# One change in four places of a spectral-gating kernel: warm-up matmuls, late tables, filter gathers and the last product

## The chip, the cores and the metric

The kernel runs on one core of a Trainium2 chip. The metric is device microseconds of one execution. Every timed execution comes with the span of the core and the mean clock that TensorE was granted (1.0 is full speed), and one execution of each kernel is kept as a full trace. Executions of a kernel can fall in a slower state; all named here are of the fast state unless the text says otherwise, and a single execution has no state of its own.

One thing has to be said at the start, because the whole reading hangs on it: after the first measurement, the five batches of experiments fell on five different chips (numbered 4, 15, 7, 12 and 1), and the kernel before is about 10 us slower on some of them than on others. The number of the first chip was not recorded. Each chip was met in one batch only, so the chip can't be told from the hour; "a chip with late marks", below, is short for both. Ratios are therefore always taken against the kernel before **on the same chip in the same rounds**.

## The reference

```python
def reference(A_x, A_w_r, A_w_i, ..., B_w_gate, B_w_up, B_w_down):   # cut
    x  = A_x                                  # [1, 2048, 640]
    xn = layernorm(x)
    X  = rfft2(xn) * (w_r + 1j * w_i)         # filter of 2048 x 321
    s  = irfft2(X)
    g  = silu((gelu(xn @ w_gate) * (xn @ w_up)) @ w_down)   # 640 -> 1536 -> 640
    return x + s * g
```

The two branches share TensorE. The feed-forward branch gives it most of its work. The spectral branch is a chain of small products with copies and multiplications between them; after its first stage it writes its data to DRAM and reads it back in another order (the *regroup*, four loads of 0.66 MB), and it multiplies by filter rows that are fetched in eight groups, G = 0 to 7.

## The kernel before

All instructions are first put in a plan (`add` with an engine, a cost, an order and what it must follow); a list scheduler then fixes the order on each engine, so a change in one place can move instructions elsewhere. The parts that the change touches:

```python
def keep_warm(e):                        # 12 dummy matmuls on constants
    place(heat, (2, 512))
    for k in range(12):
        nc.tensor.matmul(heat.tile[:, k % 2, :], lhsT=idle.tile[:, 0:P], rhs=idle.tile, ...)
...
def gather(G):                           # filter rows of group G, four gathers on GpSimd
    def go(e):
        sw.tile = WF[G % 3]              # three buffers: groups 0, 1, 2 need not wait
        for pm in range(2):              # row k, and its mirror row (2048 - k) % 2048
            for ri, wsrc in enumerate((A_w_r, A_w_i)):
                nc.gpsimd.indirect_dma_start(out=sw.tile[:, pm, ri, 0:L], in_=wsrc,
                    in_offset=bass.IndirectOffsetOnAxis(ap=LANE[:, 2 * G + pm:...], axis=0))
    W_in[G] = add(go, "POOL", ..., after=[stored[7]] + ([W_in[G - 1]] if G else []), new=[sw])
...
for k in ("ti", "i1", "im", "it"):       # late tables: SyncE, directly behind the regroup
    load_tab(k, (0, 1, seq[0]), after=[B_in["go"]])
...
# last product: two column pieces, 384 and 256 wide; per piece tanh on ScalarE, then
# (product * y), (tanh + 1) * that, + x  on VectorE, and a store
for lo, hi, tag in ((0, 384, "pg"), (384, 640, "pu")) if last else ...:
```

Of the kernel before, what the change touches and what calls it, by code (L numbers as in the profile page):

```python
# [11 lines left out]
FP32 = mybir.dt.float32  # L12
# [121 lines left out]
class Plan:  # L134
# [6 lines left out]
    def __init__(self, bufs, free):  # L141
        self.bufs, self.free = bufs, dict(free)
        self.tasks, self.slots = [], {t: [] for t in bufs}
        self.wire = 2200.0
# [84 lines left out]
def kernel(  # L229
# [33 lines left out]
    warm = consts.tile([P, 1], FP32)  # L263
    STAT = consts.tile([P, NSLAB, 12], FP32)
# [57 lines left out]
    def load_tab(k, rank=None, after=()):  # L322
        seq[0] += 1
        tab_in[k] = dma(flat(tiles[k]), tabs[k], rank or (0, -4, seq[0]), int(np.prod(tiles[k].shape)) * 2, after=after)
# [18 lines left out]
    nc.scalar.dma_start(out=X[:, 1, :], in_=xv[:, 1, :])  # L343
    nc.scalar.activation(out=warm, in_=warm, func=ACT.Gelu_apprx_tanh)
# [8 lines left out]
    def keep_warm(e):  # L353
        place(heat, (2, 512))
        for k in range(12):
            nc.tensor.matmul(heat.tile[:, k % 2, :], lhsT=idle.tile[:, 0:P], rhs=idle.tile, start=True, stop=True, skip_group_check=True)
    t = add(blank, "DVE", (330, 400), (0, -9), new=[idle])
    add(keep_warm, "PE", (12 * 430, 12 * 430), (0, -9), after=[t], new=[heat], use=[idle])
# [3 lines left out]
    load_tab("id")  # L362
    load_x(3, 4)
# [19 lines left out]
    def stats(n1, engs):  # L383
        x = X[:, n1, :]
        mean, var, rstd = MVA[:, n1, 0:1], MVA[:, n1, 1:2], RSTD[:, n1, :]
        costs = {"DVE": (1000, 1200), "ACT": (1900, 2050)}
        junk = Slot("th")

        def first(e):
            if e == "DVE":  # L390
                for g in range(2):
                    nc.vector.bn_stats(out=STAT[:, n1, 6 * g:6 * g + 6], in_=x[:, 320 * g:320 * g + 320])  # L392
                nc.vector.bn_aggr(out=MVA[:, n1, :], in_=STAT[:, n1, :].rearrange("p (g s) -> p g s", g=2))
                nc.vector.tensor_scalar_add(out=var, in0=var, scalar1=1e-5)  # L394
                return
            j = place(junk, (D,))
            nc.scalar.activation(out=j, in_=x, func=ACT.Copy, scale=-1.0 / D, accum_out=NM[:, n1, :])
            nc.scalar.activation(out=j, in_=x, func=ACT.Square, scale=1.0, bias=NM[:, n1, :], accum_out=var)

        eng = engs[0]  # L400
        t = add(first, eng, costs[eng], (2, n1), after=[x_in[n1]] + ([aps[3]] if n1 > 3 else []), new=[junk] if eng == "ACT" else [], use=[sX])
# [8 lines left out]
    def apply(n1, root, new):  # L410
# [8 lines left out]
        return add(go, "DVE", (360, 510), (1, n1, 0), hold=350 if n1 < 4 else 0, after=[root], new=[sxn] if new else [], use=[sX] if new else [sX, sxn])  # L419
# [109 lines left out]
    def gather(G):  # L529
        sw = Slot("W")  # L530

        def go(e):
            sw.tile = WF[G % 3]
            for pm in range(2):
# [4 lines left out]
        W_in[G] = add(go, "POOL", (4200, 4200), (3, G), after=[stored[7]] + ([W_in[G - 1]] if G else []), new=[sw],  # L539
# [6 lines left out]
    for k in ("ti", "i1", "im", "it"):  # L546
        load_tab(k, (0, 1, seq[0]), after=[B_in["go"]])
# [4 lines left out]
    def spectral(G):  # L552
# [34 lines left out]
        z_done = add(cp, either(1024), None, (1, 101 + 10 * G), after=[a], use=[pz, sZ])  # L587
        sE, es, firsts = Slot("ma"), [], []
# [170 lines left out]
    def gate_up(grp, t):  # L759
# [28 lines left out]
        a = add(act, "ACT", c_act(512), (0, step[0]), after=[last[id(Wg)]], new=[ge], use=[pg])  # L788
# [10 lines left out]
    def down(n1):  # L799
# [7 lines left out]
        for lo, hi, tag in ((0, 384, "pg"), (384, 640, "pu")) if last else ((0, 320, "pg"), (320, 640, "pu")):  # L807
# [13 lines left out]
            def tanh(e, lo=lo, hi=hi, ps=ps, th=th):  # L821
                place(th, (320 if not last else 384,), FP32)
                nc.scalar.activation(out=th.tile[:, 0:hi - lo], in_=ps.tile[:, 0:hi - lo], func=ACT.Tanh, scale=0.5)  # L823
# [83 lines left out]
```

## Time and profile before

| | kernel before |
|---|---|
| time, three runs before the change | 218.37 to 219.92 us, median 219.0 |
| span of the profiled run | 216.9 us |
| TensorE busy | 202.5 us, 93% of the span |
| VectorE busy | 164.0 us, 76% |
| ScalarE busy | 104.2 us, 48% |
| mean granted clock | 0.975 |

The busy shares alone say "TensorE"; they do not say where its 14 idle microseconds and its time at half clock lie. The prediction below goes through the slices, the stretches and the chain to find them. In the views PE is TensorE, PEld its weight loads, DVE VectorE, ACT ScalarE, POOL GpSimd and SP SyncE. One view that the prediction tells but does not show is GpSimd's timeline. Its columns are start, duration, engine, line, operation, output and input, and in brackets the idle time ahead of it with its cause:

```profile
43.57 1.09 POOL L536 DMA_INDIRECT WF<-in_A_w_r_dram,LANE  x1 [0.18 <-issue]
...
57.49 0.95 POOL L536 DMA_INDIRECT WF<-in_A_w_i_dram,LANE  x1 [0.30 <-issue]
```

These are the first and the last of twelve gathers that stand in a row, one every 1.25 us, from 43.6 to 58.4 us.

### The profile page before, as it was taken

To read this page: it belongs to the slowest core of one execution; us is meant where nothing else is said; L and a number is where in the kernel's file an instruction comes from. 1 tells how busy PE (TensorE), PEld (TensorE's weight loads), DVE (VectorE), ACT (ScalarE), POOL (GpSimd) and SP (SyncE) were. 2 spreads that over 40 slices of the span, in tenths; PEclk is the share of its full clock that TensorE was granted. 3 is DMA by queue.
4 is the path that set the end of the run, shared out by engine and by line. 5 is a ranking of instruction groups with operands and counts; after the bars stand their busy time and mean duration, and the time that the engine had idled before them with its cause. 6 is when DMAs were issued, how large, how long until landed. Compare 5 with 4: busy or idle time off the path is not lost.

```text
span 216.9 us, 3725 instructions
## 1 busy us (share of the span) xinstructions
PE 202.5 (93%) x1372; PEld 121.2 (56%) x1372; DVE 164.0 (76%) x342; ACT 104.2 (48%) x179; POOL 53.7 (25%) x80
## 2 busy tenths in 40 slices
PE   7699999998389999999998999999999999999990
PEld 2584444665134566567775444447776656645770
DVE  3989899981032469999977999963479999994464
ACT  5578664442022437855856434441456455542311
POOL 2432411277600000626572730000000010220000
PEclk9799999999959999999999999999999999999999
DMA  5999999689994000114323350217701231553111
GB/s 146 323 317 341 365 244 252 151 219 242 322 365 174 0 0 3 30 30 117 102 58 97 106 167 0 78 63 235 294 5 43 77 124 60 151 165 110 39 52 60
DMA packets 30913, 31.05 MB, mean 143 GB/s; under 512 B 10400, under 2 KB 27440, under 8 KB 30896
## 3 DMA queue, kind: packets, MB, share of 16 engines
q1 hardware_dynamic: 28416, 25.40, 38.8%
q0 software_dynamic: 2336, 5.26, 9.3%
q8 instruction: 10, 0.16, 0.3%
q10 hardware_dynamic: 144, 0.16, 0.2%
q14 instruction: 7, 0.06, 0.1%
HBM read 20.99 MB, written 7.86 MB: 133 GB/s over the span
## 4 chain that ended last, share of the span: by engine, by line
PE 89%; issue 4%; DVE 3%; DMA 1%; ACT 1%
PE pg L771 25%; PE pu L771 25%; PE pg L814 11%; PE pu L814 11%; PE sp L670 2%; PE sp L601 2%; PE sp L702 2%; PE sp L715 2%; PE sp L597 2%; PE sp L712 2%; PE sp L580 2%; PE sp L481 2%; DMA X<-in_A_x_dram 1%; DVE STAT L392 1%; PE sp L427 1%
## 5 line engine op out<-in xcount | busy, mean ns | idle before, releaser
L771 PE MATMUL pg<-xnT,Wg 128*128 128x512 bf16 (+1 forms) x270 | 62.6, 363 | 3.4 <-issue 2.0
L771 PE MATMUL pu<-xnT,Wu 128*128 128x512 bf16 (+1 forms) x270 | 62.1, 363 | 0.0
L783 ACT ACTIVATE ge<-pg 128x512 bf16<-128x512 f32 x48 | 28.5, 595 | 41.4 <-PE pg L771 38.6
L814 PEld LDWEIGHTS <-uT 128*128 128x128 bf16 x384 | 37.1, 98 | 17.8 <-issue 3.2
L787 DVE TENSOR_TENSOR uT<-pu,ge 128x512 bf16<-128x512 f32 x48 | 32.9, 687 | 13.1 <-PE pu L771 11.8
L771 PEld LDWEIGHTS <-Wg 128*128 128x128 bf16 x270 | 25.2, 101 | 27.1 <-issue 5.0
L771 PEld LDWEIGHTS <-Wu 128*128 128x128 bf16 x270 | 25.2, 101 | 23.1 <-issue 1.5
L814 PE MATMUL pu<-Wd,uT 128*128 128x320 bf16 (+1 forms) x192 | 32.0, 301 | 1.7 <-issue 1.7
L814 PE MATMUL pg<-Wd,uT 128*128 128x320 bf16 (+1 forms) x192 | 31.6, 301 | 0.0
L296 ACT CAST ma<-sp 128x640 bf16<-128x640 f32 (+1 forms) x29 | 22.7, 789 | 13.9 <-PE sp L715 7.3
L536 POOL DMA_INDIRECT WF<-in_A_w_r_dram,LANE x16 | 16.4, 1023 | 43.8 <-DVE mc L637 40.3
L796 POOL DMA_DIRECT2D xr<-in_A_x_dram x16 | 8.7, 548 | 71.6 <-DVE res L863 71.6
L536 POOL DMA_INDIRECT WF<-in_A_w_i_dram,LANE x16 | 16.3, 1017 | 4.9 <-issue 4.9
L829 DVE SCALAR_TENSOR_TENSOR G<-th,pg 128x320 bf16<-128x320 f32 x15 | 7.3, 484 | 12.9 <-ACT th L823 8.5
L823 ACT ACTIVATE th<-pg 128x320 f32<-128x320 f32 (+1 forms) x16 | 7.1, 444 | 19.5 <-PE pg L814 18.7
L829 DVE SCALAR_TENSOR_TENSOR G<-th,pu 128x320 bf16<-128x320 f32 x15 | 7.3, 485 | 11.4 <-ACT th L823 10.3
L406 POOL TENSOR_TENSOR RSTD<-MVA,mh 128x1 f32<-128x1 f32 x16 | 9.4, 593 | 17.7 <-DVE MVA L394 17.0
L823 ACT ACTIVATE th<-pu 128x320 f32<-128x320 f32 (+1 forms) x16 | 7.0, 437 | 10.1 <-remote 6.8
L296 ACT CAST mc<-sp 128x640 bf16<-128x640 f32 x11 | 7.2, 696 | 6.5 <-PE sp L482 3.2
L296 ACT CAST IU<-sp 128x640 bf16<-128x640 f32 x13 | 8.9, 692 | 2.4 <-PE sp L670 2.4
L392 DVE BATCH_NORM_STATS2 STAT<-X 128x6 f32<-128x320 bf16 x18 | 7.9, 481 | 2.4 <-DMA X<-in_A_x_dram 2.4
L650 DVE TENSOR_TENSOR R<-Y 64x644 bf16<-64x644 bf16 x16 | 7.8, 490 | 0.4
(81 smaller groups left out, 248.8 us busy)
## 6 DMA issues: line engine op xcount, KB each, us to landing
BU<-D SPq DMA_DIRECT2D x8, 640.0 KB
D<-mc SPq DMA_DIRECT2D x8, 320.0 KB
D<-IU SPq DMA_DIRECT2D x8, 320.0 KB
xr<-in_A_x_dram POOLq DMA_DIRECT2D x16, 160.0 KB
out_dram<-res SPq DMA_DIRECT2D x15, 160.0 KB
Wg<-in_B_w_gate_dram SPq DMA_DIRECT2D x6, 320.0 KB
Wu<-in_B_w_up_dram SPq DMA_DIRECT2D x6, 320.0 KB
Wd<-in_B_w_down_dram SPq DMA_DIRECT2D x2, 960.0 KB
```

The lines of the kernel that those rows point to most:

```text
L296: return nc.scalar.copy(out=out, in_=in_) if e == "ACT" else nc.vector.tensor_copy(out=out, in_=in_)
L392: nc.vector.bn_stats(out=STAT[:, n1, 6 * g:6 * g + 6], in_=x[:, 320 * g:320 * g + 320])
L406: nc.gpsimd.tensor_tensor(out=rstd, in0=var, in1=mh, op=ALU.pow)
L536: nc.gpsimd.indirect_dma_start(out=sw.tile[:, pm, ri, 0:L], out_offset=None, in_=wsrc, in_offset=bass.IndirectOffsetOnAxis(ap=LANE[:, 2 * ...
L650: nc.vector.tensor_tensor(out=o, in0=Yf[:, ::-3, :], in1=Yf[:, 1:3, :], op=ALU.subtract)
L771: nc.tensor.matmul(ps.tile[:, lo:hi], lhsT=w[:, c, t * P:(t + 1) * P], rhs=xnT[:, c, grp * 512 + lo:grp * 512 + hi], start=(c == 0), stop= ...
L783: nc.scalar.activation(out=ge.tile, in_=pg.tile, func=ACT.Gelu_apprx_tanh)
L787: nc.vector.tensor_tensor(out=u.tile, in0=pu.tile, in1=ge.tile, op=ALU.mult)
L796: nc.gpsimd.dma_start(out=sx.tile, in_=xv[:, n1, :])
L814: nc.tensor.matmul(ps.tile[:, 0:hi - lo], lhsT=uT[grp, t].tile[:, j * P:(j + 1) * P], rhs=Wd[:, t, lo:hi], start=(t == 0), stop=(t == 11))
L823: nc.scalar.activation(out=th.tile[:, 0:hi - lo], in_=ps.tile[:, 0:hi - lo], func=ACT.Tanh, scale=0.5)
L829: nc.vector.scalar_tensor_tensor(out=G2.tile[:, lo:hi], in0=th.tile[:, 0:hi - lo], scalar=1.0, in1=ps.tile[:, 0:hi - lo], op0=ALU.add, op1 ...
```

## The change

The intent: keep TensorE's clock up at the start (dummy matmuls paced by the landing of x, and the first slabs of x and the identity issued by three engines), keep the late tables and eight of the twelve gathers away from the regroup, and shorten the tail by cutting the last product into three column pieces. The core of the diff:

```diff
+    nc.scalar.dma_start(out=X[:, 3, :], in_=xv[:, 3, :])
+    nc.gpsimd.dma_start(out=ident, in_=tabs["id"])
...
-    add(keep_warm, "PE", (12 * 430, 12 * 430), (0, -9), after=[t], new=[heat], use=[idle])
+    t = keep_warm(6, [t])
+    t = keep_warm(4, [t, x_in[0]], 0)          # rhs is the landed slab 0
+    keep_warm(3, [t, x_in[1]], 1)              # rhs is the landed slab 1
...
             sw.tile = WF[G % 3]
+            if 0 < G < 3:
+                nc.gpsimd.tensor_copy(out=gate, in_=sB.tile[0:1, 8 * G - 8, 0:1])   # waits for regroup part 0 or 2
...
     for k in ("ti", "i1", "im", "it"):
-        load_tab(k, (0, 1, seq[0]), after=[B_in["go"]])
+        load_tab(k, (0, 1, seq[0]), after=[B_in["go"]], eng="ACT")
...
+        if G == 0:
+            for k in ("ti", "i1", "im", "it"):
+                tab_in[k].after.append(z_done)             # after the first Z eviction
...
-        for lo, hi, tag in ((0, 384, "pg"), (384, 640, "pu")) if last else ((0, 320, "pg"), (320, 640, "pu")):
+        parts = ((0, 256, "pg"), (256, 512, "pu"), (512, 640, "pg")) if last else ((0, 320, "pg"), (320, 640, "pu"))
```

Cut here: the statistics of a slab are planned in two steps instead of one, some costs of the plan are adjusted, and the last product's VectorE steps become silu, multiply, add.

More of the change, by code (lines that the diff above doesn't have):

```diff
@@ L143, in __init__ @@
         self.tasks, self.slots = [], {t: [] for t in bufs}
-        self.wire = 2200.0
+        self.wire = 2600.0
     def add(self, emit, eng, cost, rank, after=(), new=(), use=(), size=0, slow=1.0, hold=0):
@@ L263 @@
     warm = consts.tile([P, 1], FP32)
+    gate = consts.tile([1, 1], BF16)
     STAT = consts.tile([P, NSLAB, 12], FP32)
@@ L320, in load_x, with load_tab @@
             x_in[n] = t
-    def load_tab(k, rank=None, after=()):
+    def load_tab(k, rank=None, after=(), eng="SP"):
         seq[0] += 1
-        tab_in[k] = dma(flat(tiles[k]), tabs[k], rank or (0, -4, seq[0]), int(np.prod(tiles[k].shape)) * 2, after=after)
+        size = int(np.prod(tiles[k].shape)) * 2
+        if eng == "SP":
+            tab_in[k] = dma(flat(tiles[k]), tabs[k], rank or (0, -4, seq[0]), size, after=after)
+        else:
+            tab_in[k] = add(lambda e: nc.scalar.dma_start(out=flat(tiles[k]), in_=tabs[k]), "ACT", (430, 430), rank, after=after, size=size)
     def load_gu(a, b):
@@ L351, in blank, with keep_warm, go @@
         nc.vector.memset(place(idle, (512,)), 0.0)
-    def keep_warm(e):
-        place(heat, (2, 512))
-        for k in range(12):
-            nc.tensor.matmul(heat.tile[:, k % 2, :], lhsT=idle.tile[:, 0:P], rhs=idle.tile, start=True, stop=True, skip_group_check=True)
+    def keep_warm(n, after, src=None):
+        def go(e):
+            if heat.tile is None:
+                place(heat, (2, 512))
+            for k in range(n):
+                nc.tensor.matmul(heat.tile[:, k % 2, :], lhsT=idle.tile[:, 0:P], rhs=idle.tile if src is None else X[:, src, 0:512],
+                                 start=True, stop=True, skip_group_check=True)
+        return add(go, "PE", (n * 430, n * 430), (0, -9), after=after, new=[] if heat.users else [heat], use=[idle, sX] + ([heat] if heat.users else []))
     t = add(blank, "DVE", (330, 400), (0, -9), new=[idle])
-    add(keep_warm, "PE", (12 * 430, 12 * 430), (0, -9), after=[t], new=[heat], use=[idle])
+    t = keep_warm(6, [t])
     load_x(0, 1)
@@ L361 @@
     load_x(2, 3)
-    load_tab("id")
-    load_x(3, 4)
+    t = keep_warm(4, [t, x_in[0]], 0)
+    keep_warm(3, [t, x_in[1]], 1)
+    x_in[3] = tab_in["id"] = x_in[2]
     load_gu(0, 2)
@@ L385, in stats, with moments, total, square @@
         mean, var, rstd = MVA[:, n1, 0:1], MVA[:, n1, 1:2], RSTD[:, n1, :]
-        costs = {"DVE": (1000, 1200), "ACT": (1900, 2050)}
         junk = Slot("th")
-        def first(e):
-            if e == "DVE":
-                for g in range(2):
-                    nc.vector.bn_stats(out=STAT[:, n1, 6 * g:6 * g + 6], in_=x[:, 320 * g:320 * g + 320])
-                nc.vector.bn_aggr(out=MVA[:, n1, :], in_=STAT[:, n1, :].rearrange("p (g s) -> p g s", g=2))
-                nc.vector.tensor_scalar_add(out=var, in0=var, scalar1=1e-5)
-                return
-            j = place(junk, (D,))
-            nc.scalar.activation(out=j, in_=x, func=ACT.Copy, scale=-1.0 / D, accum_out=NM[:, n1, :])
-            nc.scalar.activation(out=j, in_=x, func=ACT.Square, scale=1.0, bias=NM[:, n1, :], accum_out=var)
-        eng = engs[0]
-        t = add(first, eng, costs[eng], (2, n1), after=[x_in[n1]] + ([aps[3]] if n1 > 3 else []), new=[junk] if eng == "ACT" else [], use=[sX])
+        eng = engs[0]
+        after = [x_in[n1]] + ([aps[3]] if n1 > 3 else [])
+        def moments(e):
+            for g in range(2):
+                nc.vector.bn_stats(out=STAT[:, n1, 6 * g:6 * g + 6], in_=x[:, 320 * g:320 * g + 320])
+            nc.vector.bn_aggr(out=MVA[:, n1, :], in_=STAT[:, n1, :].rearrange("p (g s) -> p g s", g=2))
+            nc.vector.tensor_scalar_add(out=var, in0=var, scalar1=1e-5)
+        def total(e):
+            nc.scalar.activation(out=place(junk, (D,)), in_=x, func=ACT.Copy, scale=-1.0 / D, accum_out=NM[:, n1, :])
+        def square(e):
+            nc.scalar.activation(out=junk.tile, in_=x, func=ACT.Square, scale=1.0, bias=NM[:, n1, :], accum_out=var)
+        if eng == "DVE":
+            t = add(moments, "DVE", (1200, 1340), (2, n1), after=after, use=[sX])
+        else:
+            t = add(total, "ACT", (870, 1000), (2, n1), after=after, new=[junk], use=[sX])
+            t = add(square, "ACT", (930, 1100), (2, n1), after=[t], use=[junk, sX])
         def root(e):
@@ L418, in go @@
                                     op0=ALU.subtract if eng == "DVE" else ALU.add, op1=ALU.mult)
-        return add(go, "DVE", (360, 510), (1, n1, 0), hold=350 if n1 < 4 else 0, after=[root], new=[sxn] if new else [], use=[sX] if new else [sX, sxn])
+        return add(go, "DVE", (360, 510), (1, n1, 0), hold=700 if n1 < 2 else 0, after=[root], new=[sxn] if new else [], use=[sX] if new else [sX, sxn])
     def turn_pe(n1, ap):
@@ L538, in go @@
                         in_offset=bass.IndirectOffsetOnAxis(ap=LANE[:, 2 * G + pm:2 * G + pm + 1], axis=0))
-        W_in[G] = add(go, "POOL", (4200, 4200), (3, G), after=[stored[7]] + ([W_in[G - 1]] if G else []), new=[sw],
+        W_in[G] = add(go, "POOL", (4200, 4200), (3, G), use=[sB] if 0 < G < 3 else [], after=[stored[7]] + ([W_in[G - 1], B_in[2 * G - 2]] if 0 < G < 3 else [W_in[G - 1]] if G else []), new=[sw],
                       size=328704, slow=1.3)
@@ L787, in mul @@
             nc.vector.tensor_tensor(out=u.tile, in0=pu.tile, in1=ge.tile, op=ALU.mult)
-        a = add(act, "ACT", c_act(512), (0, step[0]), after=[last[id(Wg)]], new=[ge], use=[pg])
+        a = add(act, "ACT", c_act(512), (0, step[0]), after=[last[id(Wg)]], new=[ge], use=[pg], hold=900 if grp == 0 and t < 2 else 0)
         u_done[grp, t] = add(mul, "DVE", c_dve(512, 1, True), (0, step[0]), after=[a, last[id(Wu)]], new=[u], use=[pu, ge])
@@ L806, in down, with finish, f1, f2 @@
         done = []
-        for lo, hi, tag in ((0, 384, "pg"), (384, 640, "pu")) if last else ((0, 320, "pg"), (320, 640, "pu")):
+        parts = ((0, 256, "pg"), (256, 512, "pu"), (512, 640, "pg")) if last else ((0, 320, "pg"), (320, 640, "pu"))
+        yg, res = Slot("yg"), Slot("res")
+        def finish(lo, hi, done, rank, first):
+            def f1(e):
+                if first:
+                    place(yg, (D,))
+                nc.vector.tensor_tensor(out=yg.tile[:, lo:hi], in0=y.tile[:, n1 % 2, lo:hi], in1=G2.tile[:, lo:hi], op=ALU.mult)
+            def f2(e):
+                if first:
+                    place(res, (D,))
+                nc.vector.tensor_tensor(out=res.tile[:, lo:hi], in0=yg.tile[:, lo:hi], in1=sx.tile[:, lo:hi], op=ALU.add)
+            t = add(f1, "DVE", c_dve(hi - lo), rank, after=[y_done[n1]] + done, new=[yg] if first else [], use=[y, G2] if first else [y, G2, yg])
+            t = add(f2, "DVE", c_dve(hi - lo), rank, after=[t, xr], new=[res] if first else [], use=[yg, sx] if first else [yg, sx, res])
+            dma(lambda: outv[:, n1, lo:hi], lambda: res.tile[:, lo:hi], (0, 0, n1), 256 * (hi - lo), after=[t], use=[res])
+        for lo, hi, tag in parts:
             ps, th, mm = Slot(tag), Slot("th"), []
@@ L821, in tanh @@
             def tanh(e, lo=lo, hi=hi, ps=ps, th=th):
-                place(th, (320 if not last else 384,), FP32)
+                place(th, (320,), FP32)
                 nc.scalar.activation(out=th.tile[:, 0:hi - lo], in_=ps.tile[:, 0:hi - lo], func=ACT.Tanh, scale=0.5)
-            a = add(tanh, "ACT", c_act(hi - lo), (0, step[0]), after=mm[-1:], new=[th], use=[ps])
-            if not last:
-                def silu(e, lo=lo, hi=hi, ps=ps, th=th):
-                    if lo == 0:
-                        place(G2, (D,))
-                    nc.vector.scalar_tensor_tensor(out=G2.tile[:, lo:hi], in0=th.tile[:, 0:hi - lo], scalar=1.0, in1=ps.tile[:, 0:hi - lo],
-                                                   op0=ALU.add, op1=ALU.mult)
-                done.append(add(silu, "DVE", c_dve(hi - lo, 1, True), (0, step[0]), after=[a] + done, new=[] if lo else [G2],
-                                use=[ps, th, G2] if lo else [ps, th]))
-            else:
-                yp, yg, res = Slot("ge"), Slot("yg"), Slot("res")
-                def e1(e, lo=lo, hi=hi, ps=ps, yp=yp):
-                    place(yp, (512,))
-                    nc.vector.tensor_tensor(out=yp.tile[:, 0:hi - lo], in0=ps.tile[:, 0:hi - lo], in1=y.tile[:, 1, lo:hi], op=ALU.mult)
-                def e2(e, lo=lo, hi=hi, yp=yp, th=th, yg=yg):
-                    place(yg, (D,))
-                    nc.vector.scalar_tensor_tensor(out=yg.tile[:, lo:hi], in0=th.tile[:, 0:hi - lo], scalar=1.0, in1=yp.tile[:, 0:hi - lo],
-                                                   op0=ALU.add, op1=ALU.mult)
-                def e3(e, lo=lo, hi=hi, yg=yg, res=res):
-                    place(res, (D,))
-                    nc.vector.tensor_tensor(out=res.tile[:, lo:hi], in0=yg.tile[:, lo:hi], in1=sx.tile[:, lo:hi], op=ALU.add)
-                b = add(e1, "DVE", c_dve(hi - lo, 1, True), (0, step[0]), after=mm[-1:] + [y_done[n1]], new=[yp], use=[ps, y])
-                b = add(e2, "DVE", c_dve(hi - lo, 1), (0, step[0]), after=[a, b], new=[yg], use=[th, yp])
-                b = add(e3, "DVE", c_dve(hi - lo), (0, step[0]), after=[b, xr], new=[res], use=[yg, sx])
-                dma(lambda lo=lo, hi=hi: outv[:, n1, lo:hi], lambda lo=lo, hi=hi, res=res: res.tile[:, lo:hi], (0, 0, n1), 81920, after=[b],
-                    use=[res])
@@ L853, in down @@
-        if last:
-            return
-        yg, res = Slot("yg"), Slot("res")
-        def f1(e):
-            place(yg, (D,))
-            nc.vector.tensor_tensor(out=yg.tile, in0=y.tile[:, n1 % 2, :], in1=G2.tile, op=ALU.mult)
-        def f2(e):
-            place(res, (D,))
-            nc.vector.tensor_tensor(out=res.tile, in0=yg.tile, in1=sx.tile, op=ALU.add)
-        t = add(f1, "DVE", c_dve(640), (2, n1), after=[y_done[n1]] + done, new=[yg], use=[y, G2])
-        t = add(f2, "DVE", c_dve(640), (2, n1), after=[t, xr], new=[res], use=[yg, sx])
@@ L866, in down, with silu @@
-        dma(lambda: outv[:, n1, :], lambda: res.tile, (0, 0, n1), 163840, after=[t], use=[res])
+            def silu(e, lo=lo, hi=hi, ps=ps, th=th):
+                if lo == 0:
+                    place(G2, (D,))
+                nc.vector.scalar_tensor_tensor(out=G2.tile[:, lo:hi], in0=th.tile[:, 0:hi - lo], scalar=1.0, in1=ps.tile[:, 0:hi - lo],
+                                               op0=ALU.add, op1=ALU.mult)
+            a = add(tanh, "ACT", c_act(hi - lo), (0, step[0]), after=mm[-1:], new=[th], use=[ps])
@@ L868 @@
+            done.append(add(silu, "DVE", c_dve(hi - lo, 1, True), (0, step[0]), after=[a] + done, new=[] if lo else [G2],
+                            use=[ps, th, G2] if lo else [ps, th]))
+            if last:
+                finish(lo, hi, [done[-1]], (0, step[0]), lo == 0)
+        if not last:
+            finish(0, D, done, (2, n1), True)
     for grp in range(4):
```

## The prediction

> **What bounds the kernel now.** I read the page first (busy shares and slices), then the chain of waits in order of time, then a table by stretches, then the timeline of two places. TensorE is busy for 93% of the 216.9 us span and the chain that ended last is 89% TensorE, so only three things can move the time: TensorE's idle time, TensorE time at half clock, and the tail after its last matmul. The slices show where those are:
>
> ```profile
> PE   7699999998389999999998999999999999999990
> DVE  3989899981032469999977999963479999994464
> PEclk9799999999959999999999999999999999999999
> DMA  5999999689994000114323350217701231553111
> ```
>
> One slice is 5.4 us. The hole is in slices 10 to 12 (54 to 65 us): TensorE falls to 3 tenths, VectorE to 0 and 3, and the clock is halved just afterwards. The first and last slices are the start and the tail. The table by stretches puts numbers on them (us busy, matmuls, clock, DMA share):
>
> ```profile
> 8.10:11.20 3.10, 3.08 (x30) 3.08 (x31) 2.82 (x7) 2.29 (x5) 0.37 (x1) 0.50 1.14 311
> ...
> 52.00:56.00 4.00, 2.04 (x13) 1.05 (x11) 0.49 (x1) 0.44 (x1) 3.02 (x4) 1.00 0.93 326
> 56.00:60.00 4.00, 1.14 (x4) 0.30 (x3) 0.00 (x0) 0.00 (x0) 1.89 (x2) 0.88 0.98 327
> 60.00:63.00 3.00, 2.71 (x9) 1.01 (x9) 1.37 (x3) 1.60 (x4) 0.00 (x0) 0.50 1.06 357
> 63.00:66.00 3.00, 3.00 (x9) 1.13 (x8) 0.69 (x1) 0.00 (x0) 0.00 (x0) 0.52 1.07 374
> ```
>
> Nobody computes from 56 to 60: neither VectorE nor ScalarE has an instruction, and TensorE starts four. The chain of waits shows what kind of wait it is:
>
> ```profile
> 50.78 3.23 issue
> 54.02 0.50 DVE G L829
> 54.56 0.81 PE pg L771 x3
> 55.37 1.02 issue
> 56.38 0.38 PE pg L771
> 56.76 1.03 issue
> 57.78 0.38 PE pg L771
> 58.16 0.35 issue
> 58.51 0.30 PE pu L814
> 58.81 1.10 issue
> ```
>
> "issue" is waiting that the profile can't name. Instruction by instruction, TensorE starts one weight load or one matmul every 0.70 us here, and ScalarE's tanh waits until 60.74 for a TensorE group whose last matmul started at 51.30. In the trace's semaphore records TensorE's completion marks come late only around here: the group that ended near 49.2 seems to be marked at 53.52 and the one of 51.6 at 60.72. Milder delays, of 0.5 to 3 us, and missing marks occur at 45 to 48, 90 to 93, 100 to 102, 107 to 116 and 123 us, and these are just the times in which GpSimd issues its indirect gathers of the filter (43.6 to 58.4, then 88 to 93, 97 to 102, 105 to 116, 120 to 125). Elsewhere, at the same DMA load (10 to 30 us at 320 to 360 GB/s, no gathers; the second regroup at 147 us), there is no such delay. So I read the hole as follows: twelve gathers in a row, backed up behind saturated DMA queues (regroup 2.6 MB, then the late tables), hold up completion signalling of every engine. That is an inference from coincidence, not something the profile states.
>
> **What the Trainium skill says.** (1) "TensorE: Matmul & The Clock Gate", Part 1: the clock is halved after an idle window of about 3.4 us and restored after a busy one, and the windows run freely. The trace agrees: half clock from 8.09 to 11.50 (3.41 us) and from 59.29 to 66.11 (two windows). (2) "DMA: Bandwidth & Descriptors", Issuing engines are not separate DMA queues: another issuing engine saves only issue time. Here the four late tables cost SyncE 2.28 + 0.53 + 0.80 + 0.76 = 4.4 us of issue, under saturation; moving them to ScalarE cannot speed the bytes. (3) Same page, Queues, rings and completion order: each DMA engine takes its queues in turn, packet by packet. So gathers get their turn beside the regroup and slow it; the trace has both moving between 54 and 63. (4) "Runtime: NRT & Kernel Launch", Instruction fetch mechanics: instructions come in 16 KiB blocks fetched ahead. TensorE's fetches in the trace are at 35.96 and 63.23, none inside the hole, so an instruction famine does not explain it.
>
> **The change, part by part.**
>
> *Warm-up and start.* Twelve dummy matmuls become 6, then 4 that wait for the first x slab, then 3 that wait for the second. Slab 3 is issued by ScalarE and the identity by GpSimd, so all four first slabs are under way about 0.9 us of issue sooner. Before, the dummies end at 5.55, TensorE does 0.45 us until 8.12, and so it meets its first 30 real matmuls (3.08 us) at half clock: full speed is 56 ns per 128 columns, 30 x 0.056 = 1.7 us, so 1.4 us are lost while it is the bound. I am not sure that the new pacing cures this: the first slab lands at 3.56, so the 7 paced ones, 0.43 us at half and 0.21 at full clock, end near 5.8, only 0.3 us later than before. But the order of VectorE's work (the second apply before the fourth slab's statistics, some 0.7 us earlier) brings real matmuls into the window before 8.1. Gain 0 to 2 us, centre 1.2.
>
> *Gathers and late tables.* Group 0's four gathers stay at about 44 to 49. Those of groups 1 and 2 now wait for regrouped data, parts 0 and 2, so they cannot stand in one row of twelve. The tables (0.86 MB; at 350 GB/s 2.5 us of all DMA engines) leave the place behind the regroup and follow the first Z eviction, when the load before was 98 GB/s falling to 0. The first product that needs the table TI runs at 91, so it loses nothing. The t2, fm and ft tables move in among the last stores. What the hole costs: the idle stretches in the chain between 53.1 and 60.6 are 1.5 + 1.0 + 1.0 + 0.35 + 1.1 + 0.3 = 5.3 us; the matmuls at half clock from 60.6 to 66.1 lose half of 5.5, 2.7 us. Together 8.0 us, all on the path, since TensorE has no idle time from 66 to 116 or from 119 to the tail. But group 1's four gathers still run while parts 1 to 3 of the regroup (2 MB, 6 us) stream, so I expect a residue: centre 1.5 us lost, gain 6.5.
>
> *ScalarE's four DMA issues.* 4 x 0.45 = 1.8 us of ScalarE if the queues are slack. From the product whose Gelu stands behind them to the reuse of its PSUM buffer TensorE has 1.08 + 1.08 + 0.45 + 1.08 = 3.7 us of other work by the new order, so mostly hidden; charge 0.3.
>
> *Last product in three pieces (256, 256, 128).* The matmul columns are the same. Before, the last matmul ends at 211.88 and VectorE's last operation at 214.19, a tail of 2.31 us in which VectorE runs six operations:
>
> ```profile
> 212.85 0.42 DVE L838 TENSOR_TENSOR ge<-pu,s 128x256 bf16<-128x256 f32 x1
> 213.19 0.35 DVE L847 TENSOR_TENSOR res<-yg,xr 128x384 bf16<-128x384 bf16 x1
> 213.45 0.42 DVE L842 SCALAR_TENSOR_TENSOR yg<-th,ge 128x256 bf16<-128x256 f32 x1
> 213.90 0.29 DVE L847 TENSOR_TENSOR res<-yg,xr 128x256 bf16<-128x256 bf16 x1
> ```
>
> Now pieces 0 and 1 end 1.3 and 0.67 us (12 x 0.056) before the last matmul. Estimated from the rows' slopes, a 128-column tanh takes 0.27, the silu 0.28, each bf16 step 0.22. By the new order VectorE does, after the last matmul, the end of piece 1's silu, a step of piece 0, two of piece 1, and three of piece 2: about 1.55 us. Gain 0.75. The last store still takes its 2.3 us.
>
> Sum: 1.2 + 6.5 - 0.3 + 0.75 = 8.1; with some luck lost to a new order of everything (the plan is rerun), 7.5. 219.0 - 7.5 = 211.5.
>
> **Rivals.** *(a) The hole only moves.* Gathers of groups 1 and 2 run beside the saturated regroup, and the path from matmul to Gelu to multiply to a free PSUM buffer (two buffers, 2.2 us each) can't hide 4 us of late signals. For: the delays follow gathers and grow with DMA load. Against: 44 to 48 has gathers at a DMA share near 0.9 and TensorE doesn't stop. It would give 215 to 217. *(b) The hole is not the gathers' but the regroup's own* (small 1280-byte pieces read just after they were written). For: the worst of it begins with the regroup's issue at 53.68. Against: ScalarE was already late at 50 to 53.5, and the second regroup at 147 does no harm. It would give about 216.5, start and tail alone. *(c) The spectral chain becomes the bound:* without the hole TensorE comes to the first regrouped product at about 62, not 71. VectorE is busy for 36 of the 42 us from 72 to 114, so the chain just fits; regrouped data issued at about 53 should be there by 61 without tables in the way. If it is late by 2 to 3 us, 213 to 214. *(d) All goes well,* clock kept and no residue: 219 - 8 - 2 - 0.75, about 208.
>
> **Range and chances.** (d) and the near side of the sum hold about half the weight, (c) and a partial (a) a quarter, full (a) or (b) a fifth. The limit of 2% is 214.6. Range 207.5 to 216.5; faster 0.74, same 0.23, slower 0.03: slower would need a new stall, as nothing on the path grows.
>
> **What would show it.** In the slices, no 3 or 4 for TensorE and no 5 for the clock between 52 and 66 us; in the chain no "issue" pieces of 1 us there; gathers in three separate sets of four; the tables' landing after 64 and no wait on them; the clock at 1.0 from 8 to 11.5 (the free windows make this the least certain); last matmul to last VectorE operation 1.4 to 1.7 us. I am wrong if TensorE still starts an instruction every 0.7 us while the regroup runs, or if it waits for regrouped data or for ScalarE behind its DMA issues.

## The result, and the profile after

The changed kernel took 213.07 us (median of four runs, 211.58 to 213.31; a fifth 213.53), the kernel before beside it 219.46 (218.37 to 223.28, four runs). The 223.28 counts as slow, being 2.2% above the fastest, and the ratio leaves it out; the three fast ones have the median 219.00 and the mean 219.10. The ratio is 0.9718, with a 95% interval from 0.9654 to 0.9781: faster. A ratio here is the mean time of one kernel's fast runs over the mean of the other's in the same rounds, so it isn't quite the ratio of the medians. The time lies inside the predicted range, 1.6 us above the predicted value. The execution that is kept as a trace was the fastest of the five (211.58 us, clock 1.0; the others took 212.84 to 213.53 us at 0.989 to 0.996), so the profile shows less than the usual loss.

The slices of the changed kernel (span 209.8 us, so one slice is 5.2 us):

```profile
PE   7899899999999779999999999999999999999992
DVE  3897989996324179999989999992366999994464
PEclk9999999999999999999999999999999999999999
DMA  6999999699589500113333251016900444542022
```

The 3 of TensorE, the 0 of VectorE and the halved clock are gone. Two new 7s stand in slices 13 and 14 (counted from 0), at 68 to 79 us. The same stretches as in the prediction (us busy for PE, PEld, DVE, ACT and POOL, instructions in brackets, then clock, DMA share, GB/s):

```profile
8.10:11.20 3.10, 3.08 (x54) 2.86 (x53) 3.03 (x10) 2.07 (x4) 0.74 (x1) 1.00 1.13 321
52.00:56.00 4.00, 4.00 (x28) 2.48 (x26) 0.97 (x2) 2.42 (x5) 0.00 (x0) 1.00 0.69 228
56.00:60.00 4.00, 4.00 (x21) 1.76 (x19) 1.87 (x3) 0.72 (x3) 0.00 (x0) 1.00 0.33 88
60.00:63.00 3.00, 3.00 (x15) 1.36 (x14) 0.69 (x1) 1.17 (x2) 1.15 (x2) 1.00 1.07 383
63.00:66.00 3.00, 3.00 (x27) 1.87 (x26) 1.92 (x2) 1.34 (x2) 2.28 (x3) 1.00 1.07 363
```

From 52 to 66 us TensorE has no idle time and full clock; at the start it does 54 matmuls in 3.1 us where it did 30. GpSimd's timeline tells what became of the gathers:

```profile
61.49 0.18 POOL L552 COPY gate<-BU 1x1 bf16<-1x1 bf16 x1 [12.13 <-DMA BU<-D]
61.83 0.97 POOL L555 DMA_INDIRECT WF<-in_A_w_r_dram,LANE  x1 [0.16 <-issue]
...
66.56 0.18 POOL L552 COPY gate<-BU 1x1 bf16<-1x1 bf16 x1
...
70.69 0.95 POOL L555 DMA_INDIRECT WF<-in_A_w_i_dram,LANE  x1 [0.31 <-issue]
```

The first gate waited 12.1 us for the regroup, as it should. The second did not wait at all: by 66.56 part 2 had landed too. So there are two rows, of four and of eight, and not three rows of four. The chain of waits of the changed kernel shows what follows directly behind the second row:

```profile
70.99 2.23 PE pg L793 x5
...
73.25 1.24 DVE zt L297
...
74.53 0.45 PE sp L619 x2
```

Five matmuls of 128x512, which take 1.08 us elsewhere in this chain, are accounted 2.23 us here, until 73.22; VectorE's copy of zt waited 2.2 us for them, and TensorE then waited 2.5 us for the copy. In the semaphore records the TensorE groups that ended at 67.3, 71.0 and 72.1 us seem to be marked at 68.8, 73.1 and 73.1. This is a smaller copy of the old hole, in a new place.

The tail, from the timelines: the last matmul ends at 205.73 and VectorE's last operation at 207.13, 1.40 us, against 2.31 before.

```profile
204.90 0.83 PE L853 MATMUL pg<-Wd,uT 128*128 128x128 bf16 x12
...
206.91 0.22 DVE L841 TENSOR_TENSOR res<-yg,xr 128x128 bf16<-128x128 bf16 x1
```

### The profile page after: what moved, and what is told of

It reads as the page before. It is cut to its first block, busy times and chain, and to the rows that moved or that the text cites.

```text
span 209.8 us, 3765 instructions
## 1 busy us (share of the span) xinstructions
PE 199.8 (95%) x1385; PEld 119.9 (57%) x1385; DVE 161.2 (77%) x340; ACT 106.2 (51%) x185; POOL 55.6 (27%) x83
## 4 chain that ended last, share of the span: by engine, by line
PE 77%; DMA 9%; DVE 6%; SPq 4%; ACT 2%; issue 1%; ACTq 0%; DVEq 0%
PE pg L793 19%; PE pu L793 19%; PE pu L853 12%; PE pg L853 12%; DMA X<-in_A_x_dram 5%; SPq L304 4%; DMA D<-mc 3%; PE sp L692 2%; PE sp L619 2%; PE sp L623 2%; PE sp L724 2%; PE sp L737 2%; PE sp L734 2%; PE sp L599 2%; DVE uT L809 1%
## 5 line engine op out<-in xcount | busy, mean ns | idle before, releaser
L793 PE MATMUL pu<-xnT,Wu 128*128 128x512 bf16 (+1 forms) x270 | 60.7, 356 | 0.0
L793 PE MATMUL pg<-xnT,Wg 128*128 128x512 bf16 (+1 forms) x270 | 60.7, 356 | 0.0
L853 PE MATMUL pg<-Wd,uT 128*128 128x320 bf16 (+2 forms) x204 | 31.7, 293 | 0.0
L853 PE MATMUL pu<-Wd,uT 128*128 128x320 bf16 (+1 forms) x192 | 31.0, 298 | 0.0
L297 ACT CAST ma<-sp 128x644 bf16<-128x644 f32 (+1 forms) x28 | 21.8, 794 | 9.2 <-PE sp L623 4.4
L862 ACT ACTIVATE th<-pg 128x320 f32<-128x320 f32 (+2 forms) x17 | 7.3, 429 | 21.6 <-PE pg L853 18.2
L867 DVE SCALAR_TENSOR_TENSOR G<-th,pg 128x320 bf16<-128x320 f32 (+2 forms) x17 | 8.0, 471 | 11.4 <-ACT th L862 10.5
L867 DVE SCALAR_TENSOR_TENSOR G<-th,pu 128x320 bf16<-128x320 f32 (+1 forms) x16 | 7.7, 482 | 6.9 <-ACT th L862 6.9
L297 ACT CAST Vt<-sp 128x640 bf16<-128x640 f32 x13 | 8.8, 693 | 5.7 <-PE sp L724 5.7
L619 PE MATMUL sp<-FT,zt 128*128 128x322 bf16 x32 | 7.0, 301 | 2.5 <-DVE zt L297 2.5
```

The lines of the kernel that those rows point to most:

```text
L297: return nc.scalar.copy(out=out, in_=in_) if e == "ACT" else nc.vector.tensor_copy(out=out, in_=in_)
L619: nc.tensor.matmul(pt[:, bank, 0:LP], lhsT=tl, rhs=FT[:, ft, :], start=True, stop=False, skip_group_check=True)
L793: nc.tensor.matmul(ps.tile[:, lo:hi], lhsT=w[:, c, t * P:(t + 1) * P], rhs=xnT[:, c, grp * 512 + lo:grp * 512 + hi], start=(c == 0), stop= ...
L853: nc.tensor.matmul(ps.tile[:, 0:hi - lo], lhsT=uT[grp, t].tile[:, j * P:(j + 1) * P], rhs=Wd[:, t, lo:hi], start=(t == 0), stop=(t == 11))
L862: nc.scalar.activation(out=th.tile[:, 0:hi - lo], in_=ps.tile[:, 0:hi - lo], func=ACT.Tanh, scale=0.5)
L867: nc.vector.scalar_tensor_tensor(out=G2.tile[:, lo:hi], in0=th.tile[:, 0:hi - lo], scalar=1.0, in1=ps.tile[:, 0:hi - lo], op0=ALU.add, op1 ...
```

## The experiments

The theory to be tested: rows of gathers hold up the completion marks of the other engines, and the gate gains by parting the rows. A completion mark is the raising of the semaphore by which an engine tells the others that an instruction is done. Rival 1: the late tables, queued behind the regroup on SyncE, made the hole. Rival 2: the regroup makes it by itself. To count late marks, I matched every TensorE and VectorE instruction that raises a semaphore with the next record of that semaphore, and called a mark late when it came over 0.25 us after the instruction's end. Where records are missing this count is too high, and a delay can come out too short: in the kernel before it puts the mark of the group that ended at 51.6 us at 53.5, while the prediction, taking marks in their order, has it at 60.72, when ScalarE's wait for it ended. So only "none" against "many" should be read from it.

**1. Undo the gate (a1_no_gate).**

```diff
-            if 0 < G < 3:
-                nc.gpsimd.tensor_copy(out=gate, in_=sB.tile[0:1, 8 * G - 8, 0:1])
```

> The changed kernel without the two little copies on GpSimd that wait for regrouped data (and without the waits that hung on them); the order on TensorE, VectorE, ScalarE and SyncE is the same, so the gathers of groups 1 and 2 follow those of group 0 at once, twelve in a row beside the regroup. Theory (rows of gathers beside busy DMA queues hold up the completion marks): TensorE's hole between 50 and 62 us comes back, in part at least, 4 to 8 us slower than the changed kernel, some 217 to 221 us. Rival 1 (the tables queued behind the regroup on SyncE made the hole) and rival 2 (the regroup makes it by itself): no hole, within 1 us of the changed kernel's 213.

**2. Put the late tables back behind the regroup (a2_tabs_sp).**

```diff
-   tab_in[k] = add(lambda e: nc.scalar.dma_start(out=flat(tiles[k]), in_=tabs[k]), "ACT", ...)
+   tab_in[k] = add(lambda e: nc.sync.dma_start(out=flat(tiles[k]), in_=tabs[k]), "ACT", ...)   # same place in the plan
```

> The changed kernel with its four late tables issued by SyncE directly behind the regroup again (the instruction order of TensorE, VectorE and GpSimd is the same, the gathers stay gated). Theory (gathers): 0 to 1 us slower than the changed kernel; the regroup's first part may land up to 1 us later, and so the gated gathers too. Rival 1 (late tables behind the regroup make the hole): the hole comes back and 4 to 8 us are lost, 217 to 221 us.

**3. The kernel before with the gate alone (a3_before_gate).**

```diff
+            if 0 < G < 3:
+                nc.gpsimd.tensor_copy(out=gate, in_=sB.tile[0:1, 8 * G - 8, 0:1])
```

> The kernel before with the two little copies on GpSimd alone, so that the gathers of groups 1 and 2 wait for the regrouped parts 0 and 2; nothing else is moved. Theory (gathers): the hole between 52 and 66 us goes, 5 to 7 us faster than before, 212 to 214 us. Rival 1 (tables) and rival 2 (regroup): the hole stays, 218 to 220 us.

**4. The kernel before without the gathers of groups 1 and 2 (a4_before_no_g12).** Its output is wrong, which doesn't matter for the time.

```diff
+            if 0 < G < 3:
+                nc.gpsimd.memset(sw.tile, 0.01)
+                return
```

> The kernel before with the eight gathers of groups 1 and 2 replaced by a fill of their buffers on GpSimd (the result is wrong on purpose). Theory (gathers): no hole, 6 to 9 us faster than before, 210 to 213 us, and TensorE's completion marks between 50 and 61 us come in time. Rivals 1 and 2: the hole stays although no gather runs after 49 us, 218 to 220 us.

These four ran on one chip, chip 4, and none of the expectations was met, because there the kernel before itself took 209.41 us (median of 39 runs, one of them slow), not 219. Results: without the gate 207.16 us, tables back 207.08 us, before with the gate 209.28 us, before without the eight gathers 209.22 us. Against before that is 0.989 [0.9874, 0.9907], 0.988 [0.9863, 0.9896], 0.9997 [0.9984, 1.001] and 1.0004 [0.9986, 1.0023]. The slices of the run without the gate:

```profile
PE   7999999999999999999999999999999999999992
...
PEclk9999999999999999999999999999999999999999
```

In that run the twelve gathers stand in a row from 43.3 to 58.9 us, as in the kernel before (the regroup is issued from 56.1 to 58.7, later than there), and there is no hole and not one late mark, on TensorE or VectorE; the records are complete as well. The other three have one late mark each. In the traces of the first measurement, TensorE had 21 late marks in the kernel before and 23 in the changed one, and VectorE 14 and 18. So the hole wasn't a property of the kernel alone. On this chip neither gathers nor tables nor the regroup make a hole, and none of the theories could be told from the others. What these runs do show: without late marks, the gate and the place of the tables are worth nothing (both undone kernels are within 0.1 us of each other, and at the ratio of the unaltered one in run 5), and the rest of the change is worth about 1.1%.

**5. The changed kernel itself as a control (e1_after_again).** No edit.

> The changed kernel itself, unaltered, as the control on whatever chip this lands on. The first batch ran on a chip where the kernel before took 209.4 us, not 219, and showed no hole and no late marks at all. Theory (the gate only helps where gathers hold up the completion marks): if the kernel before takes about 209 on this chip, the changed kernel takes about 207 (0.985 to 0.992 of it), the start and the tail alone; if before takes about 219, it takes 212 to 213.5 (0.97). Rival (the gate gains on any chip, say by shorter queues): 0.97 also where before takes 209.

It ran on chip 15, where before took 209.31 us: 206.74 us, 0.9888 [0.9866, 0.991], and no late mark. The theory holds and the rival falls: on a chip without late marks, the same change gives 1.1% and not 2.8%.

**6. Warm-up without pacing (b1_unpaced),** on the same chip.

```diff
-   ... rhs=idle.tile if src is None else X[:, src, 0:512],
+   ... rhs=idle.tile,
```

> The changed kernel with its last seven warm-up matmuls on constants instead of on the landed x slabs (13 in a row, no wait; the rest of the order is the same). Theory (pacing keeps TensorE busy through the window that decides the clock): the clock is halved near 8 us in more of the runs, 0.5 to 1.4 us slower than the unaltered changed kernel. Rival (free-running windows decide and the pacing does nothing): within 0.3 us.

It took 207.21 us, 0.9903 [0.9868, 0.9937]; the interval covers that of the control. The mean clock was 1.0 in four of its five runs and 0.996 in the fifth; the control had 0.996, 0.996, 1.0 and 0.997. But this mean counts the time after the last matmul too: in the control's trace the only half clock begins at 203.86 us, and the last matmul ended at 201.42. From 8.1 to 11.2 us both traces have 1.00. So the pacing does nothing that these runs can resolve. The rival holds.

**7. The old last product (b2_old_tail),** on the same chip. The edit puts the old two-piece code back (the removed lines of the diff's last part).

> The changed kernel with the old last product in two pieces (384 and 256 columns). Theory: the time from the end of the last matmul to the last VectorE operation goes from about 1.7 back to 2.3 us in the trace, 0.5 to 0.8 us slower than the unaltered changed kernel. Rival (the end is set by the last store anyway): no difference over 0.2 us.

It took 207.9 us, 0.9938 [0.9917, 0.9959]. The mean of its runs (208.02) less that of the control's (206.86) is 1.16 us. Its tail in the timeline:

```profile
201.00 0.82 PE L836 MATMUL pu<-Wd,uT 128*128 128x256 bf16 x6
...
203.84 0.29 DVE L869 TENSOR_TENSOR res<-yg,xr 128x256 bf16<-128x256 bf16 x1
```

From 201.82 to 204.13 is 2.31 us; the control has 1.41 (201.42 to 202.83). So 0.90 us of the 1.16 are read from the trace directly. The theory holds and was a little low.

**8. No gate again, one look on chip 15 (a1b_no_gate).**

> The kernel of run a1_no_gate once more, in the hope of a chip with late marks. If the kernel before takes about 219 here: theory says late marks and TensorE's hole between 50 and 62 us come back although tables and regroup stand as in the changed kernel, 217 to 221 us; rival (the tables' move cured it) says 213 and no hole. If before takes about 209 here: 207 and no late marks, as in a1_no_gate.

208.03 us and no late marks, as expected of a chip without them. As a single run of unknown state, it says no more.

**9. No gate again, one look (a1c_no_gate), and 10. the gathers farther apart (d1_apart).** These two met a chip with late marks, chip 7: before took 218.94 us there (218.08 to 221.46, seven runs, one of them slow). The edit of d1_apart makes group 1's gathers wait for the first Z eviction and group 2's for the first V operation:

```diff
-            if 0 < G < 3:
-                nc.gpsimd.tensor_copy(out=gate, in_=sB.tile[0:1, 8 * G - 8, 0:1])
+            if G in gate_src:
+                nc.gpsimd.tensor_copy(out=gate, in_=gate_src[G]())     # 1: sZ, 2: sV
```

> The changed kernel without the gate copies, a third time: it is here to meet a chip with late completion marks, as the one was on which the kernel before took 219 us. Two chips so far had none: before took 209.3 there and the gate made no difference. If before takes about 219 here, the theory (twelve gathers in a row, on a chip where gathers hold up the marks, make the hole) says late marks from 45 to 60 us and a TensorE hole, 217 to 221 us; the rival (moving the tables off the regroup cured it) says 213 and no hole. If before takes about 209 here, 207 to 208 and no late marks.

> A candidate that may beat both: the changed kernel with the gathers of group 1 waiting for the first Z eviction (about 66 us) and those of group 2 for the first V eviction (about 79 us), so that no eight gathers stand in a row. On a chip with late marks (before about 219): the wait of 2.5 us on zt at 72 to 75 us goes, 1.5 to 3 us faster than the changed kernel's 213, and late marks lie only in the windows of its gathers. On a chip without late marks (before about 209): nothing to gain, 206.5 to 207.5 us, within 0.4 us of the changed kernel.

Without the gate: 216.28 us, 25 late marks of TensorE, and the hole is back, in the very kernel in which tables and regroup stand as in the changed one (stretches, columns as above):

```profile
56.00:60.00 4.00, 1.70 (x9) 0.68 (x7) 0.00 (x0) 1.25 (x2) 2.85 (x3) 1.00 0.30 80
60.00:63.00 3.00, 0.43 (x2) 0.15 (x2) 0.64 (x2) 1.39 (x4) 0.00 (x0) 0.80 0.40 137
63.00:66.00 3.00, 3.00 (x10) 1.13 (x9) 0.94 (x2) 0.60 (x1) 0.00 (x0) 0.63 0.74 208
```

TensorE works 2.1 of the 7 us from 56 to 63 and the clock falls after it. The DMA engines are not even busy (share 0.30 and 0.40), and the tables are issued only later. So rival 1 falls, and with it my wording in the prediction that the gathers must stand behind *saturated* queues. Rival 2 falls by the same trace: the regroup is issued only from 62.51 to 64.94 us, when the hole is over. The time of the run is 2.6 us below the mean of before's fast runs (218.87), hardly more than the 2.5 us that start and tail are worth on chip 15: with the tables moved and the gathers left in a row, nothing of the hole is won, as far as one run of unknown state can say. The expected 217 was missed by 0.7 us, because I had not yet taken start and tail off.

With the gathers farther apart: 211.81 us, 0.9712 [0.9656, 0.9768], no better than the changed kernel's 0.9718 as far as the intervals tell; the 1.5 to 3 us that I had expected were not won. Two stretches of the changed kernel on its chip, with late marks:

```profile
66.00:76.00 10.00, 7.54 (x49) 3.97 (x47) 3.34 (x5) 2.65 (x5) 4.55 (x6) 1.00 0.51 159
...
84.00:100.00 16.00, 16.00 (x135) 11.19 (x134) 15.30 (x30) 11.82 (x17) 8.24 (x8) 1.00 0.24 64
```

and of d1_apart:

```profile
66.00:76.00 10.00, 10.00 (x75) 5.93 (x73) 5.71 (x9) 3.86 (x6) 3.35 (x4) 1.00 0.36 116
...
84.00:100.00 16.00, 13.36 (x106) 8.92 (x105) 12.66 (x23) 9.59 (x15) 11.50 (x11) 1.00 0.30 75
```

TensorE's 2.5 idle microseconds before 76 are gone, and 2.6 have appeared between 84 and 100. There the gathers of groups 2 and on now follow each other without a gap from 78.5 to over 95 us, and the longest delays of VectorE's marks, 5.0 and 4.1 us, lie at 93 to 94. Between 50 and 65 us, where no gathers run and the regroup streams (374 GB/s from 60 to 63), this run has no late mark, which speaks against rival 2 as well. Over the three kernels (changed, no gate, farther apart), the stall stands each time inside or directly behind the longest row of gathers. How much of d1_apart's stall is late marks and how much is filters fetched too late, I did not separate.

**11 and 12. No gather at all (f1_no_gather, f1b_no_gather).** All filter rows come by plain loads of the same bytes that SyncE issues; the mirror rows are simply wrong, so the result is wrong.

```diff
+        def rows(wsrc, k, steps):
+            return bass.AP(tensor=wsrc.tensor, offset=wsrc.offset + k * L, ap=[[a * L, n] for a, n in steps] + [[1, L]])
...
-                    nc.gpsimd.indirect_dma_start(...)
+                    for h in range(2):
+                        nc.sync.dma_start(out=sw.tile[64 * h:64 * h + 64, pm, ri, 0:L], in_=rows(wsrc, 8 * G + 4 * h, ((128, 16), (1, 4))))
```

> The changed kernel with every filter row loaded by plain transfers that SyncE issues, two of 64 rows for each of the four, so that GpSimd issues no gather at all (half of the rows are the wrong ones, so the result is wrong on purpose; the bytes and the buffers are the same). Theory (only gathers hold up the completion marks, and what is left between the changed kernel and its time on a chip without late marks is theirs): where the kernel before takes about 219, no late marks anywhere and 207 to 208.5 us, 0.945 to 0.952 of before. Rival (regroup and stores on such a chip hold up marks as well): late marks stay at 67 to 73 us and at 88 to 116, 211 to 214 us. Where before takes about 209, 206.5 to 208 and nothing is told apart.

> The kernel of run f1_no_gather once more (no gather at all, half of the filter rows wrong on purpose), the last run, in the hope of a chip with late marks. On a chip without them it took 209.9 us, 1.004 of before, because SyncE's filter loads held up ScalarE's table issues by some 5 us and the last store was slower. Where the kernel before takes about 219, theory (the gathers are what holds up the marks): no late marks, 209 to 211 us, 0.953 to 0.965 of before. Rival (other transfers hold them up too on such a chip): late marks remain and 213 us or more. Where before takes about 209: 209 to 210.5 again.

The first landed on chip 12, without late marks (before 208.96): 209.86 us, 1.0043 [1.0025, 1.0061], outside the 206.5 to 208 that I had expected. The second landed on chip 1, where before took 221.44 us: 209.66 us, **0.9446 [0.938, 0.9512]**, no late mark at all, and as many records as instructions or more. Its TensorE slices on chip 1:

```profile
PE   7699999999999699999999999999999999999990
```

The same kernel takes the same time on a chip of either kind. This is the direct test: take the gathers away, and the whole difference between the chips is gone, 12 us of the kernel before, in the same rounds. The rival (other transfers hold up marks too) falls.

The kernel isn't free of a cost of its own, which its chain shows on chip 1:

```profile
61.83 6.22 DMA WF<-in_A_w_i_dram
...
68.07 3.17 DMA I1T<-tab_i
...
71.25 0.04 ACT ge L805
```

ScalarE's four table issues waited for semaphores that SyncE's filter loads still held, and its next Gelu came only at 71.25; in the run on chip 12 TensorE is busy for 4.78 of the 6 us from 66 to 72. There the end after VectorE's last operation also takes 4.1 us instead of the control's 2.7. That is where its 3 us against the changed kernel on chips without late marks (209.86 to 206.74) mostly went, 1.2 + 1.5.

| kernel | without late marks: us (ratio), chip | with late marks: us (ratio), chip |
|---|---|---|
| before | 209.3 (15), 209.4 (4), 209.0 (12) | 219.0 (first measurement, chip not noted), 218.9 (7), 221.4 (1) |
| changed | 206.74 (0.9888), 15 | 213.07 (0.9718), first measurement |
| changed, no gate | 207.16 (0.989), 4 | 216.28 (one look), 7 |
| changed, gathers apart | not run | 211.81 (0.9712), 7 |
| no gathers (wrong) | 209.86 (1.0043), 12 | 209.66 (0.9446), 1 |

## Why the prediction was right, and where it wasn't

The number was right for the chip on which the change was measured. Its parts were not all right, and on the chips without late marks its verdict would have been wrong: 0.9888 is inside 2%.

- **The mechanism of the hole: right, and shown.** "An inference from coincidence", the prediction called it. The hole comes back when the gate goes (a1c_no_gate), the stall moves when the gathers move (d1_apart), and with the gathers all late marks go (f1b_no_gather). Two details of it were wrong. The queues need not be saturated, nor the regroup under way: in a1c_no_gate the hole stands at a DMA share of 0.30 and 0.40, before the regroup is issued. And the tables had no visible part in it.
- **"I expect a residue: centre 1.5 us lost, gain 6.5" (of the 8.0 that the hole costs): this is the term that was mis-sized.** On the chip with late marks the change won 219.10 - 212.91 = 6.2 us (means of the fast runs); the start and the tail, which don't need late marks, won 2.5 on chip 15 (means 209.37 - 206.86). The gathers' part is therefore about 3.7 us, not 6.5, if start and tail are worth the same on both chips. The hole itself did go, all of it; what came instead is rival (a), *the hole only moves*, in part; full (a) or (b) I had put at a fifth. I expected "three separate sets of four"; the two gates opened so close together that sets two and three became one row of eight, and TensorE lost 2.5 us behind it. The gates were tied to two regroup parts that were both there when they were asked for.
- **The cost of the hole, 8.0 us: about right, and so was the premise that the milder delays matter little.** VectorE does the same 342 operations in the same order in the trace of before and in that of a3_before_gate, which has no hole. Each operation of the first is level with its like at 46 us, 8.5 us late from 67 to 106 and 9.7 late at the end: 8.6 for the hole, 1.2 for the later gathers. The changed kernel's trace, laid on its control's (e1_after_again) in the same way, is 0.7 us late at 46, 1.0 at 66, 3.7 from 76 to 98 and 4.3 at the end: most of what it still loses to late marks, 2.6 us, stands behind the row of eight, and some 0.6 at the later gathers, which the change does not touch. Its other four runs took 1.3 to 2.0 us more than the traced one, and where they lost that, no trace tells.
- **Start, "gain 0 to 2 us, centre 1.2": of the right size, by subtraction alone.** On chip 15 the change wins 2.51 us, less the 1.16 of the tail leaves 1.35 for all the rest. The traces fit: a stretch of half clock near 8 us stands in two of the three traces of the old start (7.84 to 11.25 us in before, 9.36 to 12.77 in a4_before_no_g12, none in a3_before_gate) and in none of the eleven of the new; the first product comes at 7.82 to 8.34 us, against 8.63 to 8.85. The doubt "I am not sure that the new pacing cures this" was justified: b1_unpaced does as well without it. What does it instead, the order of the first slabs or something else in the new start, was not tested by itself.
- **ScalarE's four issues, 0.3 us: not seen.** They stand at 65.26 to 67.06 in the changed kernel, 1.7 us of issue in all, and putting them back on SyncE (a2_tabs_sp) changed nothing that these runs can resolve.
- **Tail, 0.75 us: right and a little low;** 0.90 read from the traces, 1.16 in the times.
- **Rivals (b) and (c)** fall: the regroup alone makes no late mark, and no wait on regrouped data bounded the changed kernel.
- **One reading was off:** in the trace the stretches of half clock lie 0.25 us earlier than the prediction says, at 7.84 to 11.25 and 59.04 to 65.86 us. Their lengths are as it says.

Together: 1.35 + 3.7 + 1.16 = 6.2, against the predicted 1.2 + 6.5 - 0.3 + 0.75 = 8.15. That the forecast of 7.5 was only 1.3 too high is in part luck: 0.6 us had been taken off for "luck lost to a new order", and the tail won more than expected where the gathers won less.

What stays open. Why some chips have late marks and others don't, and whether it is the chip or the hour, no run tells. On chips with late marks some semaphore records are also missing (221 for 226 instructions of TensorE in the changed kernel), and every execution here was recorded, so it isn't excluded that the recording takes part. f1b_no_gather changed two things at once, no indices and no issue by GpSimd (and the planned order with them: VectorE has 344 operations instead of 340); plain loads issued by GpSimd in the gathers' place were not tried. The traces tell a little: every kernel also issues sixteen plain loads from GpSimd (160 KB of x each). In f1b_no_gather three of them stand in a row at 43.5 to 44.7 us, and in the kernel before the last thirteen stand one at a time from 166 us on, without a late mark beside them; but no long row of them exists. The kernel before with the gate alone met no chip with late marks. And no correct kernel without gathers was run.

## What to carry to other kernels

Before explaining a stall, run the unchanged kernel on more than one chip and at more than one time: here the hole, and about three fifths of the gain (3.7 of 6.2 us), belonged to where or when the kernel ran, and one trace could not show that. When completions come late all over, ask which queue is active in just those moments, and move that queue's work to see whether the stall follows. Gating a row of transfers on data is worth only what the gates really keep apart; look at the times at which they open.

## What the Trainium skill lacked or had wrong

- No page that I read says that one and the same program can differ by 10 to 12 us from one chip to another, or from one batch of runs to another: the kernel before took 209.0 to 209.4 us on three chips, and 218.9 and 221.4 us on two others.
- "DMA: Bandwidth & Descriptors" does not say that gathers issued by GpSimd can hold up the completion marks of TensorE and VectorE: up to 2.6 and 3.1 us in the first trace by the count used here, 21 and 14 late marks, at most one a trace on two other chips (4 and 15), and none on a chip of the slow kind (chip 1) once the gathers were plain loads of SyncE (221.44 to 209.66 us).
- The same page, "Issuing engines are not separate DMA queues", says that issuing from several engines saves only issue time. It lacks the reverse, that one issuing engine can be held by another's transfers through the semaphores that a program lets them share: ScalarE's table issues and the Gelu behind them waited for SyncE's filter loads until 71.25 us in the last run.
